# One early job in plain fp32, a fixed order through the ninth unit, and paced weight loads in a gated-scan mixture-of-experts kernel

## The chip, the cores and the metric

The kernel runs on one core of one Trainium2 chip. The metric is the device time of one execution in microseconds. Before the change three runs gave 777.43 (median), 776.98 and 778.2 us.

## What is computed

A gated recurrence runs along each of 4 sequences of 3648 tokens with 256 channels, and its output goes through a two-level mixture of experts: 4 groups of 4 experts, each an MLP 256 -> 1024 -> 256. Every token goes to one of 16 experts.

```python
f = lower_bound + (1 - lower_bound) * sigmoid(f_logit);  i = 1 - f
h[t] = f[:, t] * h[t - 1] + i[:, t] * x[:, t]            # the scan; x = all h, N = 14592 rows of 256
g_idx = argmax(x @ w_group);   e_idx = argmax(x @ w_expert[g_idx])
h1 = relu(x[rows of e] @ w1[e]);  ye = h1 @ w2[e]
out[rows of e] = softmax weight of group * softmax weight of expert * ye
```

## The kernel before

**Phase one** goes over the 14592 rows in 29 units of 512 rows (`UNIT`), u0 to u28. For a unit, `p1_load` fetches 1 MB of logits and inputs into a `zt` tile (four buffers; by a DMA from SP up to u8, from ACT's queue from u9 on). ACT does a tanh (L184) and two scalings (L194, "the scaling" below); DVE multiplies (L210, or L230 in the fixed stretch) and runs two scans of 512 steps (L221, one for each half of the channels), which give the tile `h`. PE transposes `h` back to rows (L248, eight transposes in fp32), ACT copies them to a `rows` tile (L250), and PE computes the router's logits (L262, fp32, four column groups side by side) and turns them (L273). Units are routed in groups (`GROUPS`: u0; u1 and u2; u3 and u4; u5; u6; u7 and u8; then pairs): a dozen small DVE instructions find each row's expert and its place in that expert's list (`posi`), and POOL scatters the rows, 128 at a time (L343), to the lists in DRAM (`xs`).

**Early jobs** ("A", numbered 0 to 15, one for each expert) are run on the first rows of a list while phase one goes on. `EARLY` gives for each the unit after which its list is cut and the number of 128-row tiles: jobs 0 and 1 are cut at u7, jobs 2 and 3 at u9, jobs 4 and 5 at u11, each with two tiles (256 rows), the later ones with three to six. `close_early` computes the cut (`posA`), `early_rows` makes SP load the rows (`xr`). SP handles its queue in order, so a load that waits for scatters holds up all that stands behind it. 16 later jobs ("B") take the rest of the lists once phase one is done, in an order that the `order` step finds from the lists' lengths.

**A job** has these steps. `job_weights` loads the expert's 2 MB in four pieces of 128 x 1024 fp32 into `st` tiles (eight buffers). `job_split` makes two half-width copies of each piece: ACT casts it to `wh` in fp16 (L775), DVE subtracts to get the rest `wl` in bf16 (L776). `job_xt` transposes the rows on PE (L816), ACT casts them to `xh` (L821), DVE subtracts for `xl` (L822). `m1_step` does the first product in four steps for a 256-row chunk, twelve matmuls of 128 x 256 each: xh by wh, xl by wh, xh by wl (L850 to L852); ACT applies the relu and casts to `hh` (L855), DVE makes the rest `hl` (L856). `m2_step` does the second product (L869), 24 matmuls for each 128 rows, again wh by hh, wl by hh, wh by hl; ACT scales by the row's weight (L881), POOL scatters the result to the output (L882). A job of 256 rows thus has 96 matmuls of 256 columns.

**What sets the order.** The program is emitted as a list of small steps ("thunks"). The first ones (`p1_thunks`, up to the mark "begun" in u8) and the preparation of job 0 stand in a `manual_schedule` block: PE, DVE and ACT run them in the order written. After that the main loop emits a job's steps and pops steps of phase one between them (`bg_step`), at a rate that reaches each cut's mark in time, and a scheduler orders the instructions of each engine at build time; it may also move an instruction of the later part up among the written ones. In the fixed stretch a group is routed in the unit behind it (units up to u7); from u8 on the routing steps are queued and popped one at a time between the steps of the units. While running, each engine takes its instructions strictly in that order.

Of the kernel before, what the change touches and what calls it, by code (L numbers as in the profile page):

```python
# [18 lines left out]
P = 128  # L19
# [21 lines left out]
def gated_scan_moe(ctx: ExitStack, tc, zx, lower, wroute, wexp, out, S):  # L41
# [234 lines left out]
    def route_thunks(G, T, fast=False):  # L276
# [64 lines left out]
        def s7(t0, t1):  # L341
            for t in range(t0, t1):
                sc = nc.gpsimd.indirect_dma_start(  # L343
                    out=xs_v[G["t0"] + t][:, :],
                    out_offset=bass.IndirectOffsetOnAxis(ap=R["posi"][:, t:t + 1], axis=0),
                    in_=G["rows"][t // 4][0].bitcast(I32)[:, t % 4, :], in_offset=None, bounds_check=LROWS - 1, oob_is_err=False)
                for ld in early_loads:
                    tc.declare_no_dep(sc.ins, ld, reason="rows below a cut are never written again")
# [37 lines left out]
    def p1_thunks(us, groups):  # L386
# [28 lines left out]
        cut = EARLY[0][0]  # L415
# [13 lines left out]
        for u in us + [us[-1] + 1]:  # L429
            seq = []  # L430
            if u <= cut + 1:
                put(lambda u=u: (p1_load(u + AHEAD - 1), early_blanks(u + 4)))
                ending = u - 1 in ends and u <= cut
                if not ending:
                    put(lambda u=u: p1_ta(u + 1))
                if u > 0:
                    put(lambda u=u: p1_router(u - 1))
                    put(lambda u=u: logits(u - 1))
                    if u > 1:
                        put(lambda u=u: p1_gate(u))  # L440
                put(lambda u=u: p1_tb(u, 0))
                if ending:
                    bind, bound, (s1, f4x, s2, f3, f4, s6, f5, s7s) = routing(u - 1)
                    put(bind)
                    put(lambda u=u: p1_tanh(u + 1))
                    put(s1)
                    put(f4x)
                    if u > 1 and member[u - 2] == member[u - 1]:
                        put(lambda u=u: p1_back(u - 2, 0))
                        put(lambda u=u: p1_back(u - 2, 1))  # L450
                    put(s2)
                    put(f3)
                    put(f4)
                    put(lambda u=u: p1_affine(u + 1))
                    put(lambda u=u: p1_back(u - 1, 0))
                    put(lambda u=u: p1_back(u - 1, 1))
# [5 lines left out]
                elif u > cut:  # L462
                    put(lambda u=u: p1_back(u - 1, 0))
                    put(lambda u=u: p1_back(u - 1, 1))
                if u == cut:
                    put(lambda u=u: close_early(u))
                    f = lambda u=u: early_rows(u)
                    f.mark = u
                    put(f)
                f = lambda u=u: p1_tb(u, 1)  # L470
                if u == cut + 1:
                    f.mark = "begun"
                put(f)
                continue
# [13 lines left out]
            for t in seq:  # L488
                put(t)
                slot += 1  # L490
                for _ in range(2 if u <= EARLY[0][0] else 1):
# [9 lines left out]
            if u - 1 in ends:  # L501
# [10 lines left out]
                if u in cuts and u > cut:  # L512
# [37 lines left out]

    def early_rows(u):
        for mac in macros:
# [5 lines left out]
    early_loads = []  # L558

    def tail_blank(s):  # L560
        r = sync.value_load(regs["taili"][0:1, s:s + 1], min_val=PRE, max_val=(NE - 1) * LW + PRE + N)
        sync.dma_start(out=xs[bass.ds(r, 2 * P), :].rearrange("(p k) c -> p k c", k=2),
                       in_=blank[:, None, :].broadcast_to([P, 2, RW]))
# [108 lines left out]
    def make_job(kind, idx):  # L672
# [6 lines left out]
        while at < j.len:  # L679
# [13 lines left out]
            at += w  # L693
        j.wh, j.wl, j.st = {}, {}, {}
# [24 lines left out]
    def job_rows(j):  # L719
# [52 lines left out]
    def job_split(j, i):  # L772
        j.wh[i] = wp.tile([P, 1024], F16, name=f"wh{i}")
# [4 lines left out]
    def job_xt(j, pi):  # L778
# [3 lines left out]
        if c0 == 0:  # L782
# [36 lines left out]
        hi = j.xh[ch][:, :, c0:c0 + rows]  # L819
        tpv = tp[:, 0:KD * rows].rearrange("p (k w) -> p k w", k=KD)  # L820
        nc.scalar.copy(hi, tpv)  # L821
        nc.vector.tensor_tensor(out=j.xl[ch][:, :, c0:c0 + rows], in0=tpv, in1=hi, op=ALU.subtract)  # L822
# [11 lines left out]

    def m1_step(j, ch, cs):
        w = j.chunks[ch][1]
# [22 lines left out]
    def m2_step(j, ch, t):  # L859
        b, p, g = j.parts[ch][t]  # L860
        pm = bank("m2")
# [4 lines left out]
        for c in range(KF):  # L866
# [38 lines left out]
    thunks, marks = p1_thunks(list(range(NU)), GROUPS)  # L905
# [61 lines left out]
    now = [0]  # L967
# [28 lines left out]
    for mi, mac in enumerate(macros):  # L996
        q = deque()
# [88 lines left out]
```

## Time and profile before

| | |
|---|---|
| median of three runs | 777.43 us |
| the profiled execution, its own time | 776.18 us |
| its span, first to last instruction | 774.4 us |
| mean granted TensorE clock | 0.96 |
| PE busy, DVE busy, ACT busy, POOL busy | 715.7, 538.7, 461.4, 289.4 us |
| bytes moved by DMA | 151.75 MB |

The span and 1.8 us around it make up the execution's own time. A busy PE is not PE at its peak: matmuls overlap, so that the distance between the starts of two of them is what one costs. A row of the timeline reads: start, duration, engine, line, operation, output and inputs, shape, count, and in brackets how long the engine had been idle and which instruction ended that. In the windows view each engine has its busy time in the stretch and, after x, its instructions; then come the granted TensorE clock (1.00 is full speed), the share of time in which the core's 16 DMA engines were busy, and GB/s.

### The profile page before, as it was taken

How to read it: one execution, taken by the hardware profiler on the slowest of the kernel's cores; microseconds unless marked ns; L12 is line 12 of the kernel's file. 1: busy time of each engine (PE TensorE's matmuls, PEld its weight loads, DVE VectorE, ACT ScalarE, POOL GpSimd, SP SyncE). 2: the span in 40 equal slices, each digit the busy share in tenths (PEclk: the TensorE clock that was granted, in tenths of full speed). 3: DMA queues.
4: the chain of work that ended last, by engine and by line, in shares of the span. 5: the costliest groups of instructions: out<-in, count | busy, mean ns of one | idle time of the engine just before them, and what ended most of it. 6: DMA issues, size and time to landing. Idle time of an engine off the chain costs nothing.

```text
span 774.4 us, 20888 instructions
## 1 busy us (share of the span) xinstructions
PE 715.7 (92%) x8112; PEld 634.0 (82%) x8112; DVE 538.7 (70%) x1058; ACT 461.4 (60%) x824; POOL 289.4 (37%) x272
## 2 busy tenths in 40 slices
PE   2655679999999999999999999999999999999995
PEld 1434567888888888989988898999999999999995
DVE  6889899999999966865555544555564676656540
ACT  6667777987888846454455444454555465555541
POOL 3671264577556453541211222213222322232222
PEclk9955889999999999999999999999999999999998
DMA  7997879999998826378535344453563555555300
GB/s 276 355 347 262 313 245 344 328 314 354 336 311 301 271 96 185 122 238 215 123 116 126 129 99 129 114 129 118 140 173 96 166 151 173 165 164 173 86 30 24
DMA packets 93157, 151.75 MB, mean 196 GB/s; under 512 B 52417, under 2 KB 62559, under 8 KB 89728
## 3 DMA queue, kind: packets, MB, share of 16 engines
q1 hardware_dynamic: 78080, 99.90, 43.5%
q0 software_dynamic: 11424, 30.02, 11.0%
q10 hardware_dynamic: 3552, 20.48, 7.3%
q8 instruction: 64, 1.05, 0.6%
q14 instruction: 37, 0.30, 0.1%
HBM read 112.69 MB, written 38.19 MB: 195 GB/s over the span
## 4 chain that ended last, share of the span: by engine, by line
PE 56%; DVE 19%; DMA 11%; issue 7%; ACT 3%; POOL 2%; SPq 1%; POOLq 0%; DVEq 0%; ACTq 0%
PE ps_m L869 28%; PE ps_m L850 6%; DVE wl L776 6%; PE ps_m L851 6%; PE ps_m L852 6%; DMA zt<-in_zx_dram 5%; DVE h L221 4%; PE ps_p L850 3%; PE ps_p L851 3%; PE ps_p L852 3%; DVE hl L856 3%; DMA st<-in_wexp_dram 2%; DVE zt L210 2%; DMA xs<-blank 2%; POOL out_dram L882 2%
## 5 line engine op out<-in xcount | busy, mean ns | idle before, releaser
L869 PE MATMUL ps_m<-wh,hl 128*128 128x256 f16 (+2 forms) x1320 | 265.7, 251 | 4.7 <-DVE hl L856 4.6
L869 PE MATMUL ps_m<-wl,hh 128*128 128x256 bf16 (+2 forms) x1320 | 265.7, 251 | 0.1
L869 PE MATMUL ps_m<-wh,hh 128*128 128x256 f16 (+2 forms) x1320 | 265.4, 252 | 0.2 <-ACT hh L855 0.2
L869 PEld LDWEIGHTS <-hh 128*128 128x128 f16 (+2 forms) x2640 | 195.6, 99 | 23.6 <-issue 3.3
L850 PE MATMUL ps_m<-xh,wh 128*128 128x256 f16 (+11 forms) x782 | 197.4, 263 | 2.7 <-DVE hl L856 2.7
L851 PE MATMUL ps_m<-xl,wh 128*128 128x256 bf16 (+11 forms) x782 | 197.4, 262 | 1.0 <-DVE xl L822 1.0
L852 PE MATMUL ps_m<-xh,wl 128*128 128x256 f16 (+11 forms) x782 | 197.4, 262 | 0.0
L776 DVE TENSOR_TENSOR wl<-st,wh 128x1024 bf16<-128x1024 f32 x128 | 154.3, 1219 | 51.3 <-ACT wh L775 51.1
L343 POOL DMA_INDIRECT xs<-rows,posi x114 | 133.3, 1169 | 123.8 <-DVE rows L325 45.3
L882 POOL DMA_INDIRECT out_dram<-o,info x75 | 86.1, 1148 | 242.5 <-ACT o L881 214.3
L856 DVE SCALAR_TENSOR_TENSOR hl<-ps_m,hh 128x512 bf16<-128x512 f32 (+6 forms) x176 | 117.4, 670 | 70.3 <-ACT hh L855 69.9
L855 ACT ACTIVATE hh<-ps_m 128x512 f16<-128x512 f32 (+6 forms) x176 | 103.5, 588 | 72.5 <-PE ps_m L852 70.7
L775 ACT CAST wh<-st 128x1024 f16<-128x1024 f32 x128 | 132.1, 1046 | 14.1 <-PE ps_m L869 7.6
L869 PEld LDWEIGHTS <-hl 128*128 128x128 bf16 (+2 forms) x1320 | 104.6, 99 | 15.3 <-DVE hl L856 5.0
L850 PEld LDWEIGHTS <-wh 128*128 128x128 f16 x1088 | 107.2, 99 | 11.0 <-issue 1.6
L851 PEld LDWEIGHTS <-wh 128*128 128x128 f16 x1088 | 107.4, 99 | 10.5 <-issue 2.4
L852 PEld LDWEIGHTS <-wl 128*128 128x128 bf16 x1088 | 107.2, 98 | 9.4 <-issue 1.2
L882 POOL DMA_INDIRECT out_dram<-o,meta x55 | 65.5, 1192 | 111.6 <-ACT o L881 101.0
L881 ACT ACTIVATE o<-ps_m,info 128x256 f32<-128x256 f32 (+4 forms) x75 | 33.1, 441 | 83.8 <-PE ps_m L869 74.3
L850 PE MATMUL ps_p<-xh,wh 128*128 128x256 f16 (+13 forms) x306 | 73.3, 252 | 0.0
L851 PE MATMUL ps_p<-xl,wh 128*128 128x256 bf16 (+13 forms) x306 | 73.3, 252 | 0.0
L852 PE MATMUL ps_p<-xh,wl 128*128 128x256 f16 (+13 forms) x306 | 73.3, 252 | 0.0
(145 smaller groups left out, 741.2 us busy)
## 6 DMA issues: line engine op xcount, KB each, us to landing
st<-in_wexp_dram SPq DMA_DIRECT2D x128, 512.0 KB, 7.2
zt<-in_zx_dram ACTq DMA_DIRECT2D x19, 1024.0 KB, 7.5
zt<-in_zx_dram SPq DMA_DIRECT2D x7, 1024.0 KB, 9.8
xs<-blank SPq DMA_DIRECT2D x26, 258.0 KB, 4.4
xr<-xs SPq DMA_DIRECT2D x19, 258.0 KB, 6.0
xr<-xs SPq DMA_DIRECT2D x17, 129.0 KB, 4.1
xs<-rows,posi POOLq DMA_INDIRECT x114, 7.1
zt<-xs SPq DMA_DIRECT2D x8, 152.0 KB, 3.2
```

Of the source, the lines that this page charges most:

```text
L221: nc.vector.tensor_tensor_scan(out=h[:, k, c0 - a:c1 - a], data0=ff[:, k, c0 - a:c1 - a], data1=uu[:, k, c0 - a:c1 - a], initial=init, op0 ...
L343: sc = nc.gpsimd.indirect_dma_start(out=xs_v[G["t0"] + t][:, :], out_offset=bass.IndirectOffsetOnAxis(ap=R["posi"][:, t:t + 1], axis=0), i ...
L775: nc.scalar.copy(j.wh[i], j.st[i])
L776: nc.vector.tensor_tensor(out=j.wl[i], in0=j.st[i], in1=j.wh[i], op=ALU.subtract)
L850: nc.tensor.matmul(po, w1_at(j.wh, k, c), xh[:, k], start=(k == 0), stop=False)
L851: nc.tensor.matmul(po, w1_at(j.wh, k, c), xl[:, k], start=False, stop=False)
L852: nc.tensor.matmul(po, w1_at(j.wl, k, c), xh[:, k], start=False, stop=(k == KD - 1))
L855: nc.scalar.activation(hi, pv, AF.Relu)
L856: nc.vector.scalar_tensor_tensor(out=j.hl[ch][:, cs[0]:cs[-1] + 1, 0:w], in0=pv, scalar=0.0, in1=hi, op0=ALU.max, op1=ALU.subtract)
L869: nc.tensor.matmul(pm[i * q:i * q + n, 0:dw], h[ch][:, c, ts], w2_at(w, c)[:, i * dw:(i + 1) * dw], start=(c == 0 and s == 0), stop=(c == ...
L881: nc.scalar.activation(o[s, 0:dw], pm[s, 0:dw], AF.Copy, scale=lt.bitcast(F32)[s, r, 1:2])
L882: nc.gpsimd.indirect_dma_start(out=out_v[out_n[0]].rearrange("n (g d) -> (n g) d", g=g), out_offset=bass.IndirectOffsetOnAxis(ap=lt[s, r, ...
```

## The change

Three things are changed.

1. **Job 0 in plain fp32** (`RAW = 1`). Its weights are loaded straight into the tiles `wh` and `wl`, now fp32 of 128 x 512: eight DMAs of 256 KB instead of four of 512 KB. `job_split` does nothing. ACT copies the transposed rows in fp32 (two copies of 128 x 256, `xh` and `xl` now hold the two halves of the channels); each product needs one fp32 matmul where there were three; the relu writes fp32, and there is no rest to compute.
2. **The fixed order goes through u9** (`FAST = 9`), with every group that ends by then, u7 and u8 too, routed in the fixed manner. The rows of jobs 0 and 1 are asked for at u9 (`ROWS_AT`), those of jobs 2 and 3 right behind the fixed stretch. The lists behind a cut are declared free of conflicts with later scatters. (`PLAN` is empty, so the steps that `first_parts` could lay into the fixed stretch are not used.)
3. **Weight pieces** are asked for at most two ahead of what is already asked for at each split; after the preparation of job 0, pieces up to the fourteenth are asked for at once.

```diff
+FAST = 9
+PLAN = []
+ROWS_AT = {7: 9}
+RAW = 1
...
-            if u <= cut + 1:
-                put(lambda u=u: (p1_load(u + AHEAD - 1), early_blanks(u + 4)))
-                ending = u - 1 in ends and u <= cut
+            if u <= FAST:
+                put(lambda u=u: (p1_load(u + AHEAD - 1), [early_blanks(v) for v in range(u + 4 if u else 0, u + 5)]))
+                for m in [m for m, v in ROWS_AT.items() if u == v]:
+                    f = lambda m=m: early_rows(m)
...
+                ending = u - 1 in ends
...
     def job_weights(j, i):
         e = job_e(j)
+        if j.raw:
+            j.wh[i] = wp.tile([P, 512], F32, name=f"wh{i}")
+            j.wl[i] = wp.tile([P, 512], F32, name=f"wl{i}")
+            for t, c in ((j.wh[i], 2 * i), (j.wl[i], 2 * i + 1)):
+                sync.dma_start(out=t, in_=wexp[bass.ds(e * P, P), c * 512:(c + 1) * 512])
+            return
...
     def job_split(j, i):
+        if j.raw:
+            return
...
+        if j.raw:
+            for k, t in enumerate((j.xh[ch], j.xl[ch])):
+                nc.scalar.copy(t[:, 0:rows], tpv[:, k])
...
+    def raw1(j, ch, cs):
...
+        for n, c in enumerate(cs):
+            for k, x in enumerate((j.xh[ch], j.xl[ch])):
+                nc.tensor.matmul(pm[:, n * w:(n + 1) * w], (j.wh, j.wl)[c // 4][k][:, c % 4 * P:(c % 4 + 1) * P], x[:, 0:w],
+                                 start=(k == 0), stop=(k == KD - 1))
+        h, at = j.hh[ch][cs[0] // 4], cs[0] % 4
+        nc.scalar.activation(h[:, at:at + len(cs), 0:w], pm[:, 0:len(cs) * w].rearrange("p (c w) -> p c w", w=w), AF.Relu)
...
+    def raw2(j, ch, t, cs, pm):
...
+            nc.tensor.matmul(pm[0:n, 0:D], j.hh[ch][c // 4][:, c % 4, c0:c0 + n],
+                             (j.wh, j.wl)[c % 4 // 2][2 + c // 4][:, c % 2 * D:(c % 2 + 1) * D],
+                             start=(c == 0), stop=(c == KF - 1))
...
-            fetch_to(piece_index[(id(j), i)] + STG_BUFS)
+            at = piece_index[(id(j), i)]
+            fetch_to(max(at + 1, min(at + (4 if j.raw else STG_BUFS), pptr[0] + 2)))
...
-        bg_to(first)
-        start_macro(0)
-        prep = prep_thunks(macros[0][0])
         bg_to(marks["begun"])
-        for t in prep:
+        start_macro(len(PLAN))
+        for t in prep_thunks(macros[len(PLAN)][0]):
             t()
+        fetch_to(14)
+        bg_to(marks[9])
```

**How the order of instructions moves.** The tiles carry a running number; the same unit has other numbers before and after.

DVE, about the routing of u6 (the rows `mx` to `posA`) behind the first scan of u7. Before:

```order
L221 SCALAR_TENSOR_TENSOR h_591<-zt_446 128x448
L283 TENSOR_REDUCE mx_682<-Lg_673 128x20
L285 TENSOR_TENSOR ge_684<-Lg_673,mx_682 128x80
L289 SCALAR_TENSOR_TENSOR pw_688<-ge_684,pri_89 128x80
L291 TENSOR_REDUCE pm_690<-pw_688 128x20
L293 TENSOR_TENSOR oh_692<-pw_688,pm_690 128x80
```

After (line numbers of the changed kernel; `wl0_984` is the first weight split of job 1):

```order
L225 SCALAR_TENSOR_TENSOR h_599<-zt_454 128x448
L818 TENSOR_TENSOR wl0_984<-st_574,wh0_983 128x1024
L287 TENSOR_REDUCE mx_690<-Lg_681 128x20
L289 TENSOR_TENSOR ge_692<-Lg_681,mx_690 128x80
L293 SCALAR_TENSOR_TENSOR pw_696<-ge_692,pri_89 128x80
L295 TENSOR_REDUCE pm_698<-pw_696 128x20
L818 TENSOR_TENSOR wl1_988<-st_576,wh1_987 128x1024
L297 TENSOR_TENSOR oh_700<-pw_696,pm_698 128x80
```

The four weight splits of job 1, which stood behind those of job 0, now stand in the routing of u6 (the other two just before and behind its `posi`).

DVE, from u9 to the first splits. Before (u9 is `h_777`, u10 `h_878`; `wl0_814` to `xl_836` belong to job 0, `wl0_867` and `wl1_873` to job 1):

```order
L210 SCALAR_TENSOR_TENSOR zt_658<-zt_658 128x1024
L221 SCALAR_TENSOR_TENSOR h_777<-zt_658,h_680 128x512 x2
L210 SCALAR_TENSOR_TENSOR zt_775<-zt_775 128x1024
L221 SCALAR_TENSOR_TENSOR h_878<-zt_775,h_777 128x512
L776 TENSOR_TENSOR wl0_814<-st_300,wh0_813 128x1024
L776 TENSOR_TENSOR wl1_820<-st_302,wh1_819 128x1024
L776 TENSOR_TENSOR wl2_826<-st_304,wh2_825 128x1024
L776 TENSOR_TENSOR wl3_832<-st_306,wh3_831 128x1024
L822 TENSOR_TENSOR xl_836<-ps_p_837,xh_835 128x512
L824 COPY meta_844<-xr_758 128x4
L776 TENSOR_TENSOR wl0_867<-st_566,wh0_866 128x1024
L776 TENSOR_TENSOR wl1_873<-st_568,wh1_872 128x1024
```

After (u9 is `h_761`, u10 `h_840`, u11 `h_993`, u12 `zt_991` and `h_1047`; `meta_936` belongs to job 0, `xl_1060` to job 1; the routing of u7 and u8 stands ahead of these rows):

```order
L225 SCALAR_TENSOR_TENSOR h_761<-zt_666,h_688 128x512
L873 COPY meta_936<-xr_809 128x4
L225 SCALAR_TENSOR_TENSOR h_840<-zt_759,h_761 128x512
L214 SCALAR_TENSOR_TENSOR zt_797<-zt_797 128x1024
L225 SCALAR_TENSOR_TENSOR h_993<-zt_797,h_840 128x512 x2
L214 SCALAR_TENSOR_TENSOR zt_991<-zt_991 128x1024
L871 TENSOR_TENSOR xl_1060<-ps_p_1061,xh_1059 128x512
L873 COPY meta_1068<-xr_821 128x4
L225 SCALAR_TENSOR_TENSOR h_1047<-zt_991,h_993 128x512 x2
```

The splits and the `xl` of job 0 are gone from DVE; u9 to u12 follow one another with one `xl` among them.

ACT, about the first column steps of job 0. Before, the scaling of u11 (`zt_876`) stands between the relu of job 0's first step (`hh_847`) and that of its second:

```order
L855 ACTIVATE hh_847<-ps_m1_849 128x512
L250 COPY rows_883<-ps_p_904 128x2x256
L274 COPY Lg_792<-ps_p_911 128x80
L184 ACTIVATE zt_876<-zt_876 128x1024
L250 COPY rows_924<-ps_p_925 128x2x256
L194 ACTIVATE zt_876<-zt_876,mid_85,half_83 128x512 x2
```

After (`zt_797` is u11, `zt_991` u12; `xh_927` and `xl_928` are job 0's rows, `hh_975` its relu):

```order
L198 ACTIVATE zt_797<-zt_797,mid_85,half_83 128x512
L867 COPY xh_927<-ps_p_929 128x256
L867 COPY xl_928<-ps_p_929 128x256
L198 ACTIVATE zt_797<-zt_797,mid_85,half_83 128x512
L256 COPY rows_997<-tokno_102 128x4
L178 DMA zt_1045<-in_zx_dram 128x2048
L895 ACTIVATE hh_975<-ps_m1_977 128x512
L254 COPY rows_997<-ps_p_998 128x2x256
L269 COPY rs_1016<-ps_p_1007 128x128
L895 ACTIVATE hh_975<-ps_m1_1018 128x512
L254 COPY rows_997<-ps_p_1034 128x2x256
L278 COPY Lg_1041<-ps_p_1042 128x80
```

Right behind these rows stands the scaling of u12 (`zt_991`), and with it the DVE row `zt_991` above: both now come behind the relu of job 0's second column step. On PE, fp32 matmuls (L892 in the first product, L927 in the second) stand where job 0's triples stood; of the 7590 matmul rows of the changed kernel, those behind about the first fifth stand in the same order as before.

More of the change, by code (lines that the diff above doesn't have):

```diff
@@ L414, in p1_thunks, with back, wave @@
         put(lambda: p1_ta(us[0]))
-        cut = EARLY[0][0]
+        backed = set()
+        def back(v):
+            if v not in backed:
+                backed.add(v)
+                put(lambda v=v: p1_back(v, 0))
+                put(lambda v=v: p1_back(v, 1))
+        def wave(u, n):
+            while parts and n and parts[0][0] <= u:
+                put(parts.pop(0)[1])
+                n -= 1
         def routing(v):
@@ L441, in p1_thunks @@
                 put(lambda u=u: p1_tb(u, 0))
+                wave(u, 1)
                 if ending:
@@ L461, in p1_thunks @@
                         put(f)
[L462 to L465, printed above, removed]
-                    put(lambda u=u: close_early(u))
-                    f = lambda u=u: early_rows(u)
-                    f.mark = u
+                    wave(u, 1)
+                elif u > 7:
+                    wave(u, 1)
+                    back(u - 1)
+                if u in cuts and u - 1 in ends:
+                    put(lambda u=u: close_early(u))
+                put(lambda u=u: p1_tb(u, 1))
+                wave(u, 1 if u < FAST else 99)
+                if u == FAST:
+                    f = lambda: None
+                    f.mark = "begun"
                     put(f)
[L470 to L473, printed above, removed]
+                    for v in [v for v in sorted(cuts) if v <= FAST and v not in ROWS_AT]:
+                        f = lambda v=v: early_rows(v)
+                        f.mark = v
+                        put(f)
                 continue
@@ L490, in p1_thunks @@
                 slot += 1
-                for _ in range(2 if u <= EARLY[0][0] else 1):
+                for _ in range(1):
                     if not hold:
@@ L511, in p1_thunks @@
                 put(bind)
-                if u in cuts and u > cut:
+                if u in cuts:
                     rs.append(lambda u=u: close_early(u))
@@ L549, in close_early @@
                     j.pos = posA
+    asked = set()
     def early_rows(u):
+        asked.add(-u)
         for mac in macros:
@@ L558, in gated_scan_moe @@
     early_loads = []
+    scatters = []
     def tail_blank(s):
         r = sync.value_load(regs["taili"][0:1, s:s + 1], min_val=PRE, max_val=(NE - 1) * LW + PRE + N)
-        sync.dma_start(out=xs[bass.ds(r, 2 * P), :].rearrange("(p k) c -> p k c", k=2),
-                       in_=blank[:, None, :].broadcast_to([P, 2, RW]))
+        bl = sync.dma_start(out=xs[bass.ds(r, 2 * P), :].rearrange("(p k) c -> p k c", k=2),
+                            in_=blank[:, None, :].broadcast_to([P, 2, RW]))
+        for _, sc in scatters:
+            tc.declare_no_dep(bl.ins, sc, reason="blank rows begin behind a list's last row")
     def order():
@@ L693, in make_job @@
             at += w
+        j.raw = kind == "A" and idx < RAW
         j.wh, j.wl, j.st = {}, {}, {}
@@ L763, in job_rows @@
                     early_loads.append(ld.ins)
+                for u, sc in scatters:
+                    if u >= EARLY[j.idx][0]:
+                        tc.declare_no_dep(ld.ins, sc, reason="rows scattered behind a cut lie above it")
             j.rows.append(r)
@@ L865, in m2_step @@
         ts = slice(c0, c0 + n)
-        for c in range(KF):
+        if j.raw:
+            raw2(j, ch, t, range(KF // 2 if begun else 0, KF), pm)
+        for c in range(0 if j.raw else KF):
             for s, (h, w) in enumerate(((j.hh, j.wh), (j.hh, j.wl), (j.hl, j.wh))):
@@ L904, in gated_scan_moe, with first_parts, begin @@
     live = [0]
-    thunks, marks = p1_thunks(list(range(NU)), GROUPS)
+    def first_parts():
+        out = []
+        for (j,), u in zip(macros, PLAN):
+            half = {}
+            def begin(j=j, half=half):
+                half[0] = bank("m2")
+                raw2(j, 0, 0, range(KF // 2), half[0])
+            fs = [lambda j=j: job_xt(j, 0)]
+            fs += [lambda j=j, cs=cs: m1_step(j, 0, cs) for cs in j.cols[0]]
+            fs += [begin, lambda j=j, half=half: m2_step(j, 0, 0, half[0])]
+            out += [(u, f) for f in fs]
+        return out
+    thunks, marks = p1_thunks(list(range(NU)), GROUPS, first_parts())
     bgq = deque(thunks)
@@ L966, in gated_scan_moe @@
                 due[-1] = (at - work(mac) // 2, marks["order"])
-    now = [0]
+    now = [sum(work(mac) for mac in macros[:len(PLAN)])]
     credit = [0.0]
```

44 lines of the change are left out of this document (31 added, 13 removed).

## Prediction

> **What bounds the kernel now.** I read the table of stretches first, then the timeline of each engine about the points where its character changes.
>
> ```profile
> 60.00:100.00 40.00, 27.08 (x213) 20.68 (x214) 35.69 (x56) 27.74 (x54) 9.37 (x10) 0.67 0.82 276
> 100.00:130.00 30.00, 24.37 (x214) 19.12 (x213) 29.76 (x60) 25.09 (x45) 14.67 (x13) 0.87 0.88 297
> 130.00:275.00 145.00, 143.72 (x1493) 127.82 (x1491) 141.98 (x259) 118.63 (x220) 89.00 (x70) 1.00 0.91 313
> 275.00:750.00 475.00, 474.54 (x5713) 431.81 (x5711) 279.55 (x555) 245.87 (x420) 135.32 (x121) 1.00 0.50 139
> ```
>
> From 130 us on PE is busy without a break. Up to 275 us DVE is nearly full too (141.98 of 145 us), behind that it has half its time free: the last 475 us are PE's alone. Between 60 and 130 us PE has gaps and a lowered clock (0.67, 0.87), and DVE is busy 35.69 of 40 and 29.76 of 30 us. So what is done for phase one and the first jobs is paced by DVE, and PE runs after it until about 130 us. Two places show who waits:
>
> ```profile
> 95.56 0.40 PE L869 MATMUL ps_m<-wh,hl 128*128 128x256 f16 x1 [4.64 <-DVE hl L856]
> 273.70 0.27 PE L850 MATMUL ps_m<-xh,wh 128*128 128x256 f16 x1 [0.92 <-DVE hl L856]
> 283.50 0.69 DVE L856 SCALAR_TENSOR_TENSOR hl<-ps_m,hh 128x512 bf16<-128x512 f32 x1 [3.85 <-ACT hh L855]
> ```
>
> At 95.56 PE had waited 4.64 us for a rest (`hl`) of job 0 that DVE came to late; at 273.70 it waits for DVE a last time (0.92 us). At 283.50 DVE waits 3.85 us for a relu, that is for PE: there DVE is ahead by about that much. What moves the end is therefore when PE and DVE have the first jobs and phase one behind them, by whichever is later of the two.
>
> **Work taken from DVE.** Job 0 loses its splits, its `xl` and its `hl`:
>
> ```profile
> 67.65 4.61 DVE L776 TENSOR_TENSOR wl<-st,wh 128x1024 bf16<-128x1024 f32 x4
> 72.17 0.69 DVE L822 TENSOR_TENSOR xl<-ps_p,xh 128x512 bf16<-128x512 f32 x1
> 76.31 0.67 DVE L856 SCALAR_TENSOR_TENSOR hl<-ps_m,hh 128x512 bf16<-128x512 f32 x1
> ```
>
> The four splits take 4.61 us, `xl` 0.69, `hl` 0.67 for each of four steps: 4.61 + 0.69 + 2.68 = **8.0 us**. They lie between 67 and 105 us in a queue that is full until 275 us, so nothing hides them now, and without them DVE ends phase one up to 8.0 us earlier. ACT loses four casts and one of `xh` and gains two half-size copies:
>
> ```profile
> L775 ACT CAST wh<-st 128x1024 f16<-128x1024 f32 x128 | 132.1, 1046 | 14.1 <-PE ps_m L869 7.6
> ```
>
> Four casts of 1.05 us, 4.2 us. ACT is busy 25.09 of 30 us where DVE is busy 29.76, so DVE's work covers this and I count nothing; without that cover it would be up to 4 us more of gain.
>
> **Work added to PE.** A matmul of 256 columns in 16 bits costs the distance of two starts:
>
> ```profile
> 85.81 0.27 PE L869 MATMUL ps_m<-wh,hh 128*128 128x256 f16 x1
> 85.92 0.27 PE L869 MATMUL ps_m<-wl,hh 128*128 128x256 bf16 x1
> 81.75 0.60 PE L248 MATMUL ps_p<-ident,h 128*128 128x128 f32 x4
> 82.28 0.64 PE L262 MATMUL ps_p<-h,wr 128*32 128x128 f32 x16
> ```
>
> That is 0.109 us (85.81 to 85.92), with a record 0.16 us longer than the distance; job 0's 96 matmuls cost 10.5 us. The trace has no plain fp32 matmul of this shape. From below: four fp32 transposes of 128 columns take 0.60 us, less the tail 0.44, 0.11 each; 256 columns at that rate are 0.218 us, and 32 matmuls 7.0 us, 3.5 us less than now. From above: the router's eight matmuls leave 16 records, two for each. Four of them run side by side, so 0.64 less the tail, some 0.45 us, are four rounds of 0.11 for 128 columns; 256 columns in two records would cost 0.436 us, and the job 14.0 us, **3.5 us more**. I take the upper value, because the router's matmuls multiply, as job 0's will, and a transpose does not. The Trainium skill, "FP8 and Floating Point Precision", section "TensorE Precision Notes", has true fp32 in four passes through the array. By that rule the job would come to 4 x 32 x 0.109 = 14.0 us too, and the transposes' rate would not apply; no row before the change settles it.
>
> It counts in PE's own path, below.
>
> **When job 0 starts.** Before, its rows and first matmul were here:
>
> ```profile
> 56.47 1.81 POOL L343 DMA_INDIRECT xs<-rows,posi  x1 [0.30 <-DMA xs<-rows,posi]
> 61.14 1.03 POOL L343 DMA_INDIRECT xs<-rows,posi  x1 [0.30 <-issue]
> 65.87 2.73 SPq L760 DMA_DIRECT2D xr<-xs  x4
> 68.17 1.32 PE L816 MATMUL ps_p<-ident,xr 128*128 128x128 f32 x4 [5.72 <-DMA xr<-xs]
> 71.30 0.82 PE L850 MATMUL ps_m<-xh,wh 128*128 128x256 f16 x3
> ```
>
> u6's four scatters leave POOL from about 56.5 to 61.1 us, 1.28 us apart, in a queue without a pause; SP's load follows 4.7 us behind the last, and PE has the rows 2.3 us later. After the change the routing of u6 has job 1's four splits in it, 4.61 us that move up from later. DVE's idle time there,
>
> ```profile
> 54.68 0.16 DVE L543 SCALAR_TENSOR_TENSOR posA<-runoff,taken 128x2 int32<-128x2 f32 x1 [1.65 <-ACT runoff L379]
> 57.46 2.46 DVE L221 TENSOR_TENSOR_SCAN h<-zt,h 128x512 f32<-128x512 f32 x2
> 60.10 1.23 DVE L210 SCALAR_TENSOR_TENSOR zt<-zt 128x1024 f32<-128x1024 f32 x1 [0.17 <-ACT zt L194]
> ```
>
> takes up 1.65 us of them, so u8's last scan ends not at 57.46 + 2.46 = 59.9 but at 62.9 us. The scatters slip by about 1 us at most, so rows are there near 70 us. But ACT's copies for job 0 stand behind the tanh of u12, whose load can be asked for only when u8 has freed its buffer:
>
> ```profile
> zt<-in_zx_dram ACTq DMA_DIRECT2D x19, 1024.0 KB, 7.5
> 61.90 1.06 ACT L184 ACTIVATE zt<-zt 128x1024 f32<-128x1024 f32 x1 [1.69 <-DMA zt<-in_zx_dram]
> 62.99 0.81 ACT L194 ACTIVATE zt<-zt,mid,half 128x512 f32<-128x512 f32 x1
> 38.21 0.57 ACT L250 COPY rows<-ps_p 128x512 f32<-128x512 f32 x1
> ```
>
> 62.9 + 7.5 us to landing + 1.06 for the tanh + two row copies of 0.57 and small ones (about 1.5) + a scaling of 0.81 and two copies of half the size (about 0.8) gives **74.6 us** for the first matmul of job 0, against 71.3 before.
>
> **PE's path.** Up to the first matmul of job 3,
>
> ```profile
> 132.29 0.27 PE L850 MATMUL ps_m<-xh,wh 128*128 128x256 f16 x1
> ```
>
> PE has to do job 0 (14.0), job 1 (10.5), the first product of job 2 (5.2), three row transposes (0.5 each), and for u9 to u13 eight transposes, the router and one more (8 x 0.109 + 0.45 + 0.11 = 1.4 each): 14.0 + 10.5 + 5.2 + 1.5 + 7.1 = 38.3 us at full clock. The clock is the other part:
>
> ```profile
> 60.00:70.00 10.00, 4.01 (x17) 3.35 (x17) 8.46 (x8) 8.12 (x14) 1.86 (x2) 0.50 0.65 222
> 70.00:80.00 10.00, 9.56 (x79) 6.92 (x78) 9.32 (x15) 7.24 (x16) 0.00 (x0) 0.65 0.91 316
> ```
>
> It was half at 60 to 70 us and 0.65 on average at 70 to 80, so it came back near 77 us, some 5.7 us behind 71.3. If job 0 again runs 5.7 us at half clock, half of that is lost, 2.8 us. 74.6 + 38.3 + 2.8 = 115.7 us, and 1.4 us more for u14, which stood ahead of job 3 before: 117.1. Against 132.3 PE could be **15.2 us earlier**, if it never waited. The gain comes from the second product of job 0, which needs no `hl` any more (the 4.64 us above), and from the rows of jobs 2 and 3:
>
> ```profile
> 90.36 1.24 POOL L343 DMA_INDIRECT xs<-rows,posi  x1 [28.20 <-ACT hh L855]
> 104.33 2.69 SPq L760 DMA_DIRECT2D xr<-xs  x4
> ```
>
> Before, POOL idled 28.20 us until the routing of u7 and u8 was through, and these rows were asked for at 104.33. Now that routing ends near 73 us; eight scatters at 1.28 us and 4.7 us later is 88 us, 16 us earlier and ahead of their use.
>
> **DVE's path.** 8.0 us less work. Waits that go: 1.65 us (filled, above), 1.23 us at the load of u10, whose place is now filled by routing,
>
> ```profile
> 65.12 1.23 DVE L210 SCALAR_TENSOR_TENSOR zt<-zt 128x1024 f32<-128x1024 f32 x1 [1.23 <-ACT zt L194]
> 81.19 0.19 DVE L331 TENSOR_TENSOR both<-ps_p,runoff 128x32 f32<-128x32 f32 x1 [1.59 <-PE ps_p L309]
> ```
>
> and 1.59 us for the routing product: 4.5 us. One wait comes. The routing of two units in the fixed manner takes, first and last row of fourteen:
>
> ```profile
> 35.12 0.29 DVE L283 TENSOR_REDUCE mx<-Lg 128x40 f32<-128x160 f32 x1
> 39.79 0.29 DVE L377 TENSOR_REDUCE posi<-sc 128x8 int32<-128x128 f32 x1
> ```
>
> 5.0 us with 1.17 us of waiting in it, so 3.8, and a cut 0.3. DVE reaches the multiplication of u12 at 62.9 + 3 x 3.7 (u9 to u11, 1.23 + 2.46 us each) + 4.1 = 78 us. But ACT scales u12 behind the relu of job 0's second column step. Each step has four of the matmuls: at half clock the first takes 3.5 us, the second between 1.7 and 3.5, with 1.1 us of transposes between them: 81 to 83 us, and then a relu, two copies and the two scalings, 2.8 us: 84 to 86 us. DVE waits 6 to 8 us, and job 1's `xl` and all behind it with it; I take **6 us**, since a load that lands at 7.5 us by the median had the engines less free than they are then. Bounds: nothing, if the clock is up at once and the load early; 9 us, if both steps run at half clock and the load is a little late. Sum for DVE: 8.0 + 4.5 - 6 = 6.5 us earlier, between 3.5 and 12.5.
>
> **Weight loads.** The bytes are the same. Job 0's pieces take four more issues by SP, ahead of u6's load:
>
> ```profile
> 19.53 2.81 SPq L769 DMA_DIRECT2D st<-in_wexp_dram  x4
> 22.46 14.53 DMA zt<-in_zx_dram
> 30.00:40.00 10.00, 5.60 (x44) 4.29 (x45) 8.35 (x20) 5.85 (x14) 7.83 (x7) 0.80 1.04 394
> st<-in_wexp_dram SPq DMA_DIRECT2D x128, 512.0 KB, 7.2
> ```
>
> Four issues take 2.81 us. The load behind them took 14.53 us because the DMA engines were full (share 1.04); a later request finds the same bytes ahead of it and lands at the same time. I count nothing; with that cover gone it is 2.8 us. The six pieces asked for together behind job 0's rows are needed from about 88 us on, in a stretch whose DMA share was 0.82: nothing, and if one came late, at most its time to landing, 7.2 us.
>
> **Sum.** PE could be 15.2 us earlier, DVE 6.5; both are nearly full until 275 us, so the smaller decides: 776.18 - 6.5 = 769.7 for the profiled execution, a span of 768. The median of the runs is 1.25 us above the profiled one, so I predict **771 us**.
>
> **Rivals.**
>
> *PE decides alone* (chance 0.13). DVE's lead at 283.50, 3.85 us, is spare, and with the new wait small the gain is 10 to 13 us: 764 to 767 us. Against it: DVE has 3 us free in 145.
>
> *The new wait eats the gain* (0.18). If DVE waits 9 us for u12 and the early issues cost 2.8 us, 8.0 + 4.5 - 9 - 2.8 leaves 0.7 us, and the time lies between 773.5 and 778 us. For it: the in-order wait is certain, only its length is open.
>
> *A late job 0 holds up DVE* (0.15), and the kernel is slower. Place: the scaling of u12 in ACT's order, behind job 0's second relu. Every microsecond by which job 0's first matmul comes later than 74.6 is one on DVE's wait. It decides from the point where the wait reaches 8.0 + 4.5 = 12.5 us, that is where u12 is scaled at about 91 us instead of 85. It would come about if u12's load, for which ACT stands still ahead of job 0's copies, takes as long as the one at 22.46 did, 14.5 us in place of 7.5: job 0 starts at 81.6, the wait is 13 us, and the time is 0.5 us above the old one; with both steps at half clock (1.8 us more) and with u6's 2.8 us it is 779 to 783. Against it: the DMA share at 60 to 70 us was 0.65, not 1.04. The Trainium skill, "TensorE: Matmul & The Clock Gate", section "The HAM clock gate", has the clock released after about 3.4 us of sustained work. By that rule the half clock would cost job 0 1.7 us, not 2.8; its section "PE-mode transpose" says that transposes do not count as busy in the same way, which would hold the second step at half clock too.
>
> *The paced loads do it* (inside the other cases). If asking for pieces in pairs were what helps, the scales and scans between 60 and 130 us would wait less for loads; those waits are 1.23 us at 65.12 in DVE's rows and little else, so it has no more to give than that.
>
> **Chances.** Gain of 4 to 10 us, my forecast: 0.52, 767 to 773.5 us. PE alone 0.13. Gain eaten 0.18, of which half lies within 0.2% (1.6 us, about what a measurement of this kernel can tell from no change). Slower 0.15. Something larger, 0.02. Faster by over 0.2%: 0.52 + 0.13 + 0.08 + 0.02 = 0.75; the same 0.11; slower 0.14. The range from 764 to 780 takes in the first three cases and the near end of the fourth.
>
> **What would show it.** In the new profile: no split of job 0 on DVE; job 0's matmuls near 75 us with two records each, 0.22 us apart, or one if the lower bound is right; a wait of DVE for ACT's scaling of u12, at about 79 us, of some 6 us; loads of rows for jobs 2 and 3 near 88 us; job 3's first matmul between 118 and 126 us; DVE's last full stretch ending near 268 instead of 275 us. I am wrong if job 0's first matmul comes behind 80 us, if DVE has more than 10 us of waits between 60 and 100 us, or if PE shows gaps behind 130 us that it did not have.

## The result, and the profile after

The changed kernel takes **789.02 us** (median of four runs, 787.12 to 790.75) against 777.37 before: ratio 1.0148, 95% interval 1.0123 to 1.0173, 11.6 us slower. The forecast was 771, with 764 to 780 as its range.

| | forecast | before | after |
|---|---|---|---|
| span of the profiled execution | 768 | 774.4 | 786.9 |
| u12's load asked for | 62.9 | 71.49 | 70.84 |
| job 0's first matmul | 74.6 | 71.30 | 83.0 |
| DVE's waits, 60 to 100 us | 6, for u12's scaling alone | 3.4 | 12.6, of it 3.54 for u12's scaling |
| rows of jobs 2 and 3 asked for | 88 | 104.33 | 92.51 |
| job 3's first matmul | 118 to 126 | 132.29 | 123.44 |
| rows of job 4 asked for | no term | 123.39 | 133.74 |

The same stretches of the table of windows as before (per engine busy time and, after x, instructions; then granted clock, DMA share, GB/s):

```profile
60.00:100.00 40.00, 25.98 (x200) 20.32 (x201) 26.65 (x44) 22.80 (x47) 11.06 (x12) 0.73 0.86 282
100.00:130.00 30.00, 28.50 (x258) 24.27 (x256) 29.46 (x59) 25.40 (x48) 14.45 (x11) 1.00 0.93 293
130.00:275.00 145.00, 132.47 (x1360) 115.38 (x1359) 132.58 (x240) 111.43 (x207) 85.68 (x69) 0.98 0.90 296
275.00:750.00 475.00, 471.73 (x5560) 428.61 (x5560) 284.81 (x563) 246.58 (x423) 135.08 (x120) 1.00 0.51 144
```

Between 100 and 130 us PE is now busy 28.50 of 30 us at full clock (before 24.37 at 0.87): the gain that was forecast for the first jobs is there. It is lost on both sides of that. From 60 to 100 us DVE does 26.65 us of work instead of 35.69, and from 130 to 275 us PE stands still for 12.5 us and DVE for 12.4; before, it was 1.3 and 3.0.

**From 60 to 100 us**, all of DVE's rows with a wait, in order of time:

```profile
71.48 0.32 DVE L287 TENSOR_REDUCE mx<-Lg 128x40 f32<-128x160 f32 x1 [4.52 <-ACT Lg L278]
81.77 0.16 DVE L567 SCALAR_TENSOR_TENSOR posA<-runoff,taken 128x2 int32<-128x2 f32 x1 [4.50 <-ACT runoff L384]
91.87 1.23 DVE L214 SCALAR_TENSOR_TENSOR zt<-zt 128x1024 f32<-128x1024 f32 x1 [3.54 <-ACT zt L198]
```

All three wait for ACT, so the next view is ACT's timeline with SP's (ACTq and SPq are the queues in which these engines issue DMAs):

```profile
65.16 0.27 ACT L269 COPY rs<-ps_p 128x128 f32<-128x128 f32 x1 [0.42 <-PE ps_p L266]
67.33 2.73 SPq L791 DMA_DIRECT2D xr<-xs  x4
70.84 0.33 ACTq L178 DMA_DIRECT2D zt<-in_zx_dram  x1
71.22 0.23 ACT L278 COPY Lg<-ps_p 128x80 f32<-128x80 f32 x1 [5.79 <-DMA xr<-xs]
79.56 1.06 ACT L188 ACTIVATE zt<-zt 128x1024 f32<-128x1024 f32 x1 [4.57 <-DMA zt<-in_zx_dram]
83.00 1.22 PE L892 MATMUL ps_m<-xh,wh 128*128 128x256 f32 x2
```

ACT's copy at 71.22 takes the logits from PE, yet the view names the load of job 0's rows as what ended its wait. What stood there is the row ahead of it: the issue of u12's load. A semaphore is a counter that a landed DMA raises and that a later instruction waits for. In the program as built, each DMA of SP and ACT signals on one of eight of them, dealt out in turn, and is issued only when the one eight before it has landed. u12's load is the 46th, so it waits for the 38th, the second of the loads of job 0's rows:

```
ACT  L178 DMA zt_991<-in_zx_dram 128x2048 [waits DMAHW5_49,DVE_49]
SP   L791 DMA xr_809<-xs 128x258 [waits DMAHW5_49]
```

ACT's whole queue stood from 65.4 to 70.8 us until rows had landed that it does not read. The Trainium skill, "DMA: Bandwidth & Descriptors", section "Anatomy of one DMA — SWDGE (gpsimd) path", says that a semaphore wait of a DMA takes place on the sequencer that issues it, before dispatch; the 5.79 us agree. Then the load had to come (79.56), which ACT awaited ahead of job 0's copies and of the `runoff` at 81.77 above, and job 0 began at 83.0.

**From 130 us on**, PE's gaps of over 1 us up to 275 us in its timeline, 11.5 us together:

```profile
135.96 1.32 PE L861 MATMUL ps_p<-ident,xr 128*128 128x128 f32 x4 [5.09 <-DMA xr<-xs]
155.50 0.27 PE L914 MATMUL ps_m<-xh,wh 128*128 128x256 f16 x1 [1.86 <-DVE hl L920]
178.34 0.22 PE L914 MATMUL ps_m<-xh,wh 128*128 128x128 f16 x1 [2.10 <-DVE hl L920]
189.00 0.48 PE L861 MATMUL ps_p<-ident,xr 128*128 128x128 f32 x2 [2.43 <-DMA xr<-xs]
```

And ahead of the first of them and behind it, DVE, POOL and SP in order of time:

```profile
109.73 0.37 DVE L343 TENSOR_REDUCE posi<-sc 128x8 int32<-128x128 f32 x1
112.50 1.25 POOL L347 DMA_INDIRECT xs<-rows,posi  x1 [24.52 <-ACT hh L919]
127.06 0.97 POOL L347 DMA_INDIRECT xs<-rows,posi  x1 [0.30 <-issue]
133.74 2.69 SPq L791 DMA_DIRECT2D xr<-xs  x4
145.34 0.69 DVE L920 SCALAR_TENSOR_TENSOR hl<-ps_m,hh 128x512 bf16<-128x512 f32 x1 [6.58 <-ACT hh L919]
```

The same two steps, `posi` and the load of the rows, before the change:

```profile
101.86 0.39 DVE L339 TENSOR_REDUCE posi<-sc 128x8 int32<-128x128 f32 x1
123.39 3.05 SPq L760 DMA_DIRECT2D xr<-xs  x4
```

PE waits 5.09 us for the rows of job 4. They go through the routing of u9 and u10 (`posi` at 109.73, before at 101.86), eight scatters and a load asked for at 133.74, 10.35 us later than before. DVE then waits 6.58 us for PE, and phase one, whose steps stand between the jobs' in each queue, waits with both.

One matmul carries the sum: the last one before that waited for DVE, at 273.70. After:

```profile
284.38 0.27 PE L914 MATMUL ps_m<-xh,wh 128*128 128x256 f16 x1 [1.16 <-DVE hl L920]
```

10.68 us later. It is the same matmul: from it to the last one there are 5975 records before and after, of the same operations in the same order. Nearly all that is missing to the 12.5 us of the spans is a gap of 1.68 us at 684.34 that the view puts down to nothing it shows (last section).

### The profile page after: what moved, and what is told of

The parts are those of the page before. It is cut to its first block, busy times and chain, and to the rows that moved or that the text cites. A ratio compares the mean times of both kernels' runs of the same rounds, so it can differ in the third digit from the quotient of the medians.

```text
span 786.9 us, 20828 instructions
## 1 busy us (share of the span) xinstructions
PE 717.1 (91%) x8089; PEld 635.1 (81%) x8089; DVE 531.0 (67%) x1046; ACT 458.2 (58%) x822; POOL 289.7 (37%) x272
## 4 chain that ended last, share of the span: by engine, by line
PE 63%; issue 11%; DVE 10%; DMA 9%; POOL 4%; ACT 2%; SPq 0%; POOLq 0%; DVEq 0%; ACTq 0%
PE ps_m L944 28%; PE ps_m L914 7%; PE ps_m L915 7%; PE ps_m L916 7%; DMA zt<-in_zx_dram 4%; DVE wl L818 3%; POOL out_dram L957 3%; PE ps_p L914 3%; PE ps_p L916 3%; PE ps_p L915 3%; DMA xr<-xs 2%; DVE h L225 2%; DVE hl L920 2%; PE ps_p L252 2%; DMA xs<-rows,posi 1%
## 5 line engine op out<-in xcount | busy, mean ns | idle before, releaser
L944 PE MATMUL ps_m<-wl,hh 128*128 128x256 bf16 (+4 forms) x1304 | 261.2, 251 | 1.7 <-issue 1.7
L944 PE MATMUL ps_m<-wh,hl 128*128 128x256 f16 (+4 forms) x1304 | 261.4, 251 | 0.0
L944 PE MATMUL ps_m<-wh,hh 128*128 128x256 f16 (+4 forms) x1304 | 261.0, 251 | 0.0
L914 PE MATMUL ps_m<-xh,wh 128*128 128x256 f16 (+11 forms) x766 | 191.7, 260 | 6.8 <-DVE hl L920 6.8
L915 PE MATMUL ps_m<-xl,wh 128*128 128x256 bf16 (+11 forms) x766 | 191.6, 260 | 0.3 <-DVE xl L871 0.3
L916 PE MATMUL ps_m<-xh,wl 128*128 128x256 f16 (+11 forms) x766 | 191.6, 259 | 0.0
L818 DVE TENSOR_TENSOR wl<-st,wh 128x1024 bf16<-128x1024 f32 x124 | 149.8, 1220 | 53.8 <-ACT wh L817 53.6
L920 DVE SCALAR_TENSOR_TENSOR hl<-ps_m,hh 128x512 bf16<-128x512 f32 (+9 forms) x172 | 114.8, 670 | 78.5 <-ACT hh L919 78.0
L919 ACT ACTIVATE hh<-ps_m 128x512 f16<-128x512 f32 (+9 forms) x172 | 101.1, 588 | 66.3 <-PE ps_m L916 64.6
L944 PEld LDWEIGHTS <-hl 128*128 128x128 bf16 (+4 forms) x1304 | 102.9, 99 | 10.1 <-issue 0.2
```

Of the source, the lines that this page charges most:

```text
L818: nc.vector.tensor_tensor(out=j.wl[i], in0=j.st[i], in1=j.wh[i], op=ALU.subtract)
L914: nc.tensor.matmul(po, w1_at(j.wh, k, c), xh[:, k], start=(k == 0), stop=False)
L915: nc.tensor.matmul(po, w1_at(j.wh, k, c), xl[:, k], start=False, stop=False)
L916: nc.tensor.matmul(po, w1_at(j.wl, k, c), xh[:, k], start=False, stop=(k == KD - 1))
L919: nc.scalar.activation(hi, pv, AF.Relu)
L920: nc.vector.scalar_tensor_tensor(out=j.hl[ch][:, cs[0]:cs[-1] + 1, 0:w], in0=pv, scalar=0.0, in1=hi, op0=ALU.max, op1=ALU.subtract)
```

## The experiments

Why the rows of job 4 are late can be counted in the code. `bg_step` pops steps of phase one between the steps of the jobs (a job of two row tiles has ten). Before, the steps of phase one up to the rows of job 4 were 72 when job 0 began, pulled hard by the due time of the rows of jobs 2 and 3, and were done when 18 job steps had been issued. After, the fixed stretch holds more and 52 are left, but no due time is near, and they are spread over 24 job steps.

- **Theory A**: the stop of ACT's queue at u12's load.
- **Theory B**: the order, in which the routing of u9 and u10 stands six job steps later.
- **Theory C**: the fp32 job itself.
- **Theory D**: DVE is full, so that pulling phase one forward only moves the wait.

Each set ran on another chip. The kernel before took 811.57 and 812.87 us on those of the first two sets, 776.85 and 776.84 on those of the last two; ratios are to the kernel before on the same chip, and the changed kernel itself was timed only for the result above. Single profiled executions differ from the median of their kernel by up to 2.2 us in the last two sets, by up to 10.3 us in the first two.

**First set: one suspect taken away at a time.**

```diff
 ahead10:                 ahead11:                 split0:
-        fetch_to(14)     -        fetch_to(14)    -RAW = 1
+        fetch_to(10)     +        fetch_to(11)    +RAW = 0
 order8:
-FAST = 9
+FAST = 8
-ROWS_AT = {7: 9}
+ROWS_AT = {7: 8}
-        fetch_to(14)
-        bg_to(marks[9])
```

With two weight pieces ahead of it u12's load is the 44th DMA and waits for u10's load, which is about to land by then; with three it is the 45th and waits for the first load of job 0's rows.

> Two weight pieces instead of six are asked for behind job 0's rows (the other four follow behind the rows of jobs 2 and 3), so that the load of u12 no longer shares its semaphore with a load of job 0's rows. Theory A (the stop of ACT's queue at that load is the cause: u12 was asked for at 70.84 instead of about 65, DVE had 12.6 us of waits between 65 and 92, and phase one and the rows of job 4 on came 10 us late): u12 asked for before 66, job 0's first matmul near 76, job 4's rows asked for 5 to 7 us earlier than 133.7, time 782 to 785. Theory B (jobs 0 to 3 stand too far ahead of phase one in the new order, whatever u12 does): job 0 starts earlier, PE then stands longer for job 4's rows, time 787 to 791. Theory C (the fp32 job's extra 3.5 us on PE and little else): 788 to 790.

> Three weight pieces instead of six behind job 0's rows; one more than in the run beside it, which puts u12's load back on the semaphore of a load of job 0's rows. Theory A: the stop of ACT's queue stays, u12 asked for near 70, time 787 to 791 as in the changed kernel. Theory B and C: the same as the run with two pieces, within 1 us. If the pacing of weights itself matters: both runs differ from the changed kernel in the same way.

> The fixed order ends with the eighth unit again and the routing of u7 and u8 is spread over job 0 and 1 as before; the fp32 job and the paced pieces stay. Theory A: no stop of ACT's queue (u11 and u12 are on other semaphores), so at most the time before: 770 to 778. Theory B: 770 to 778 too, since the order is what it blames. Theory C (the fp32 job): 781 or more, because PE has 3.5 us more to do and nothing else went.

> Job 0 split in 16 bits again (32 casts and splits' worth of work back on ACT and DVE: 8.0 us on DVE, 3.5 us less on PE), the new order and the paced pieces stay. u12's load comes onto another semaphore with it. Theory A: without the stop DVE gets back about 9 us of waits and has 8 us more of work: 786 to 791. Theory B (order): PE starves for job 4's rows all the same, and DVE has more to do: 788 to 796. Theory C (the fp32 job): 776 to 779.

Measured: ahead10 1.0116 (1.0052 to 1.018), ahead11 1.0144 (1.0097 to 1.0191), order8 1.0028 (0.9996 to 1.006), split0 1.0153 (1.0096 to 1.021). C falls as the main cause: with the splits back the loss is still there, and with the fp32 job in the old order most of it is gone (1.0014 when it was measured again, below). In ahead10's trace ACT asks for u12's load 1.08 us behind u11's (72.33 and 71.25); in ahead11's it stands 5.26 us until the rows of job 0 have landed. That is what the semaphores foretold, but the intervals of the two ratios overlap, so these two runs do not show what the stop costs. Most of the loss goes with the order.

**Second set: the order mended by one number.**

```diff
 pull18 (pull10: 10 in place of 18):
+    due.append((18, marks[11]))
     now = [sum(work(mac) for mac in macros[:len(PLAN)])]
 pull18_ahead10, pull10_ahead10: the same, and fetch_to(10)
 order8_split0: order8 and RAW = 0
```

In pull18 job 4's rows are reached at job step 17.

> The changed kernel with one more entry in the planner's list of due times: the rows of job 4 are due at step 18 of the jobs' steps (they came at step 24 in the changed kernel and at step 18 in the kernel before). Theory B (the new order lets the routing of u9 and u10 stand six job steps later, so job 4's rows come too late and PE runs dry near 130 us): job 4's rows are asked for 5 to 8 us earlier against job 1's matmuls, PE's gap of about 5 us ahead of job 4 goes, ratio to the kernel before 1.002 to 1.008. Theory D (DVE is full until 275 us, so pulling phase one forward only moves the wait to the jobs): the gap moves, ratio 1.011 to 1.016 as in the changed kernel.

> The same with two weight pieces in place of six behind job 0's rows, so that ACT's queue does not stop at u12's load either. Theory A and B together: 0.3% less than the run beside it, ratio 0.998 to 1.005. Theory B alone: the same as the run beside it within 0.2%. Theory D: 1.008 to 1.014.

> Job 4's rows due at step 10 instead of 18, two weight pieces. Theory B: as good as step 18 or slightly better, as long as PE does not wait for jobs 1 and 2 instead: 0.996 to 1.004. Theory D: DVE's work for phase one delays the rests of jobs 1 and 2 by what it brings the rows forward: 1.006 to 1.014.

> Order of before and job 0 split again; only the pacing of weight pieces is left, and in this order it moves nothing on any engine. All theories: the time before within 0.3%. It serves as the trace of the order before on this chip, beside which the fp32 job in the same order (ratio 1.0028) can be read: if the fp32 job gains DVE time, job 1's matmuls stand later here than there.

Measured: pull18 1.0114 (1.0073 to 1.0155), pull18_ahead10 0.9938 (0.99 to 0.9975), pull10_ahead10 1.0281 (1.024 to 1.0322), order8_split0 1.002 (0.9985 to 1.0056). The due step alone came out as D has it, not as B; both edits together did better than A and B foresaw, against D. So at step 18 the two runs do not agree. Pulling too far costs 3.4% against step 18, more than D gave it. One edit alone against both had to be measured where the times scatter less.

**Third set: the two edits apart and together, five rounds.**

> The kernel with both edits (job 4's rows due at step 18, two weight pieces behind job 0's rows) once more, beside the two that have one edit each. If the two edits add up: about 1.2% less than the changed kernel, ratio to the kernel before 0.993 to 1.003. If its 0.9938 was luck: 1.005 or more.

> Only the due step (the stop of ACT's queue stays). By the times of rows (cut 17's rows 6 us later in the trace than with both edits): ratio 0.6 to 0.9% above the run with both, so 1.001 to 1.008. If the due step does nothing by itself: 1.011 to 1.016.

> Only the two weight pieces (job 4's rows stay at step 24). By the times of rows in the trace (cut 17's rows 10 us later than with both edits): ratio 1.2% above the run with both, so 1.006 to 1.014. If ACT's stop was the cause by itself: the same as with both edits.

> Job 0 split again in 16 bits (8.0 us more of work on DVE, 3.5 us less on PE), the new order, job 4's rows due at step 18; u12's load is on another semaphore, so ACT's queue does not stop at it. If the fp32 job is worth its 8 us of DVE once the rows come in time: 0.5 to 1% above the run with both edits. If the splits of job 0 lay in the shadow of the load of its rows (as 6.3 us of waiting for that load in DVE's queue in the run with the old order and the fp32 job suggest): within 0.3% of it.

| job 4's rows at step | ACT stops at u12's load (5.8 us) | ACT does not stop for the rows |
|---|---|---|
| 24 | 1.0148 (1.0123 to 1.0173), the changed kernel | 1.01 (1.0081 to 1.0119), ahead10_b |
| 17 | 1.0054 (1.0034 to 1.0074), pull18_b | 0.9991 (0.9977 to 1.0006), pull18_ahead10_b |

The edits add up: the stop costs 0.48% or 0.63%, the late rows 0.94% or 1.09%; together 1.57%, all of the loss. The changed kernel's number in this table is that of the result, the other three are of this set. The 0.9938 of the second set was not seen again. The common matmul, in one execution of each, points the same way; ahead10_b, pull18_b and pull18_ahead10_b:

```profile
279.14 0.27 PE L914 MATMUL ps_m<-xh,wh 128*128 128x256 f16 x1 [1.16 <-DVE hl L920]
```

```profile
276.13 0.27 PE L914 MATMUL ps_m<-xh,wh 128*128 128x256 f16 x1 [1.28 <-DVE hl L920]
```

```profile
270.34 0.27 PE L914 MATMUL ps_m<-xh,wh 128*128 128x256 f16 x1 [1.28 <-DVE hl L920]
```

From 284.38, two pieces in place of six take off 5.24 us, the due step 8.25, both 14.04. The two pieces take away the stop, but not only that: u12's load, which then stands behind fewer bytes, also lands 7.0 to 7.4 us after it is asked for in place of 8.7 and 9.1. No run separates the two, so the 0.48% or 0.63% is the price of both. In pull18_ahead10_b, ACT, DVE, SP and PE at the places shown above:

```profile
66.14 0.33 ACTq L178 DMA_DIRECT2D zt<-in_zx_dram  x1
75.72 0.16 DVE L567 SCALAR_TENSOR_TENSOR posA<-runoff,taken 128x2 int32<-128x2 f32 x1 [3.17 <-ACT runoff L384]
86.43 1.23 DVE L214 SCALAR_TENSOR_TENSOR zt<-zt 128x1024 f32<-128x1024 f32 x1 [4.16 <-ACT zt L198]
118.93 0.27 PE L914 MATMUL ps_m<-xh,wh 128*128 128x256 f16 x1 [2.47 <-DVE hl L920]
122.86 2.69 SPq L791 DMA_DIRECT2D xr<-xs  x4
```

The load is asked for at 66.14, job 4's rows at 122.86, and PE's longest wait behind 100 us is 2.47 us for a rest. At the common matmul this kernel is 3.36 us ahead of the one before; it gives back 1.4 us behind that point (last section). pull18_split0 has 1.0033 (1.0018 to 1.0048): once the rows come in time, the fp32 job is worth 0.42%, 3.3 us, between the two cases that were expected. The pair also differs in the pieces asked for, six and two; pull18_split0 has no stop either, so without the fp32 job the mended order is 0.33% slower than the old one. (In the two traces the common matmul lies 8.36 us apart, 278.70 against 270.34, but the one of pull18_split0 is the longest of its eight executions.)

**Fourth set: the fp32 job alone, and both sides of step 18.** (`order8_b` is `order8`; the other two have 21 and 15 in place of 18, with `fetch_to(10)`.)

> The fp32 job in the order of before, alone. Forecast's sum (8.0 us less on DVE, of which little is lost): ratio 0.990 to 0.996. If job 0's splits lay in the shadow of the load of its rows: DVE waits about 4 to 6 us for that load at job 0's copy of its row numbers, and the ratio is 0.997 to 1.003.

> Both edits, with job 4's rows due at step 21 in place of 18. If a trade: PE's gaps for the rests of job 2 (2.63 us near 116 at step 18) shrink, a gap for job 4's rows of 1 to 3 us comes near 128; ratio 0.995 to 1.003, no worse than at 18. If lateness of rows alone counts: halfway to the run at step 24, 1.002 to 1.008.

> The same at step 15. If a trade: longer gaps for the rests of jobs 1 and 2, ratio 1.003 to 1.015 (step 10 gave 1.028 on another chip). If lateness of rows alone counts: below the run at step 18, 0.994 to 0.999.

Measured: order8_b 1.0014 (0.9997 to 1.0031). DVE in its trace, behind u9's scans:

```profile
61.01 2.47 DVE L225 TENSOR_TENSOR_SCAN h<-zt,h 128x512 f32<-128x512 f32 x2
70.78 0.17 DVE L873 COPY meta<-xr 128x4 int32<-128x4 int32 x1 [7.29 <-DMA xr<-xs]
```

DVE does not split job 0's weights and waits 7.29 us for its rows instead; the common matmul stands at 272.39, 1.31 us earlier than before. Behind it this execution loses 4.2 us (last section), so what the job gains ahead of that point does not reach the end. pull21_ahead10 has 0.9997 (0.9982 to 1.0012), pull15_ahead10 1.0028 (1.0016 to 1.0041). At 21 PE's wait of 2.47 us for a rest is gone (the longest for one is 1.25 us), and 1.35 us for the rows of job 4 have come, as a trade would have it. At 15 PE waits for the other side, for a cast of ACT ahead of job 2's first product:

```profile
113.61 0.58 PE L914 MATMUL ps_m<-xh,wh 128*128 128x256 f16 x2 [6.07 <-ACT xh L870]
```

So it is a trade between late rows and late jobs. Of the steps tried 18 and 21 are best and cannot be told apart, and no version was faster than the kernel before a second time.

## Why the prediction was wrong

- **Work taken from DVE** (8.0 us, "nothing hides them now"): the work went, the sentence was wrong. In the old order the four splits lay where DVE would otherwise wait for job 0's rows; the row at 67.65 and the load asked for at 65.87 both stood in the prediction. Alone the fp32 job gains nothing that can be measured (order8_b: 7.29 us of waiting in place of the splits), in the mended order 0.42%. That DVE was busy there did not show that it was late there.
- **Work added to PE** (3.5 us by the upper value): right. In PE's timeline after, each row below is one fp32 matmul with its two records; between their starts lie 0.43 us, and 32 make 13.8 us, forecast 14.0.

```profile
92.96 0.59 PE L892 MATMUL ps_m<-xl,wl 128*128 128x256 f32 x2
93.39 0.59 PE L892 MATMUL ps_m<-xh,wl 128*128 128x256 f32 x2
```

- **When job 0 starts** (74.6 us): the step that u12's load "can be asked for only when u8 has freed its buffer" named one of its two conditions. The other, the semaphore shared with a load of job 0's rows, held it to 70.84. Without it job 0 starts at 76.95 (pull18_ahead10_b), 2.4 us behind the forecast; there the load was asked for at 66.14, although u8's scans had ended at 63.8, since its semaphore is then that of u10's load. Half clock was forecast for 5.7 us from job 0's first matmul, a loss of 2.8 us: after 83.0 us the clock came up at 85.4, a loss of 1.2, and in pull18_ahead10_b it took 3.6 us, a loss of 1.8:

```profile
77.00:80.60 3.60, 3.60 (x12) 2.78 (x10) 3.50 (x5) 0.74 (x2) 2.83 (x3) 0.50 0.93 284
80.60:84.00 3.40, 3.40 (x26) 2.80 (x25) 1.67 (x2) 2.04 (x5) 2.03 (x3) 0.99 0.93 330
```

  Here the 3.4 us of the Trainium skill ("TensorE: Matmul & The Clock Gate", section "The HAM clock gate") lie nearer than the 5.7 us taken from the rows before, counted from job 0's first matmul.
- **DVE's waits** (6 us, between 0 and 9): the wait that was forecast, for u12's scaling, came, but was 3.54 us with the stop and 4.16 without it. The others had no term: 4.52 us behind the stop itself and 4.50 for the `runoff` that ACT reaches behind u12's load, 12.6 in all. Without the stop they are 0.46 and 3.17, with 1.07 at 95.55 for PE, 8.9 in all.
- **Weight loads** (nothing): wrong. The six issues behind job 0's rows moved u12's load to the semaphore of job 0's rows, and the load took 1.4 to 2.1 us longer to land than behind two pieces; together that cost 0.48% to 0.63%.
- **PE's path and the sum** (PE 15.2 us earlier, DVE 6.5, "the smaller decides"): this step failed most. Job 3's first matmul came at 123.44, inside the 118 to 126 of the forecast, and there the working stopped; that the head start lasts was taken from DVE being full until 275 us. But the planner had spread the next routing over 24 job steps instead of 18, and PE ran dry on job 4's rows: 0.94% to 1.09%. The sum also has no term for the 1.8 us that are lost behind the common matmul.
- **The rivals**: "a late job 0 holds up DVE" (0.15, 779 to 783 us) had the place right, and job 0 began at 83.0 where it had 81.6; its cause, a slow load, was not what happened in the main: the load was asked for 7.9 us later than forecast and took 8.7 us, not 14.5. With the rows in time this much alone gives 781.1 us (pull18_b); the rest, up to 789, no rival had.

Of what was to show the prediction wrong, all three came: job 0 behind 80 us, over 10 us of DVE's waits between 60 and 100, gaps of PE behind 130.

## What to carry to other kernels

A forecast of a new order has to follow each chain to its next consumer, past the place where work is saved: here the step at which the rows of job 4 are asked for decided more than all the work counted. Work that stands in front of a wait can be free, as the splits of job 0 were; before counting its removal as gain, ask what the engine would wait for instead. And when DMAs are added or moved, list what each later DMA issue of every queue waits for, since a shared semaphore can stop an engine that has nothing to do with the transfer.

## What was not expected of the hardware

In each of the 13 traces of kernels with the fp32 job PE stands once at nearly the same place, 1345 to 1353 matmul records from the last one, among matmuls of 64 columns four to a row, with nothing in the profile that ended the wait: 1.68 us in the changed kernel, 1.13 to 2.42 us in the third and fourth set, 0.69 to 1.51 us in the first two. In the four traces without the fp32 job there is no such gap at that place (in pull18_split0 there is one of 0.82 us at 700.58). From the common matmul to the last one the changed kernel and the fp32 kernels of the last two sets take 1.4 to 2.1 us longer than the kernel before; in order8_b it is 4.2 us, since there the granted clock was also 0.72 from 675 to 680 us, behind the gap at 673.07. So the place goes with the fp32 job, as a cost that the forecast has not. What it is stays open: the profile names neither weights nor rests as late there, and no experiment was made on it. In the changed kernel:

```profile
682.44 0.22 PE L944 MATMUL ps_m<-wh,hh 128*32 128x64 f16 x4
684.34 0.21 PE L944 MATMUL ps_m<-wl,hh 128*32 128x64 bf16 x4 [1.68 <-issue]
```
